# Attention, routed experts and a feed-forward block on one core: a threshold summed over all partitions, a new order in the last two batches, two id tiles and four result buffers

## The chip, the cores and the metric

The kernel runs on 1 core of one Trainium2 chip. The metric is the device time of one execution in microseconds (us); the median of the runs counts. The engines are named as in the profile: PE (TensorE, matmuls), DVE (VectorE), ACT (ScalarE), POOL (GpSimd) and SP (the queue that issues most DMAs); ACT and POOL issue DMAs too.

## The reference, cut to what matters

```python
def _attn_ref(q, k, v):                 # (8 batches, 8 heads, 576 tokens, 64)
    q_s = exp(q - max over d) / sum     # softmax over the head dimension
    k_s = exp(k - max over s) / sum     # softmax over the tokens
    kv = einsum('bhsd,bhse->bhde', k_s, v)
    return einsum('bhsd,bhde->bhse', q_s, kv)

def _moe_ref(x, w_gate, w_output_gate, w1, w2):   # x: 4608 tokens x 512, 8 experts
    logits = x @ w_gate
    e_idx = np.argmax(logits, axis=1)             # one expert for a token
    ...
    for e in range(E):
        mask = e_idx == e
        h = np.maximum(x[mask] @ w1[e], 0.0)      # 512 -> 1024
        ye = h @ w2[e]                            # 1024 -> 512
        out[mask] = gate_w[mask, None] * eom[mask, e, None] * ye

def _moe2_ref(x, w_in, w_out):                    # 512 -> 2048 -> 512
    r = np.maximum(x @ w_in, 0.0)
    return (r * r) @ w_out
```

The inputs are drawn from a seed. Drawn with the reference's own default seed, the experts get 1151, 0, 551, 25, 588, 577, 0 and 1716 tokens, and all 1151 of expert 0 are among the first 2304 tokens (batches 0 to 3).

## The kernel before, in words

**Front.** Eight batches of linear attention, two by two (a pair has 9 groups of 128 tokens). For batch n, `x_t` transposes and exponentiates q (PE, then ACT), `x_mm` multiplies by the batch's kv and the gate weights (PE, then two ACT copies), and `kv_mm`, `kv_t`, `kv_m` prepare the next batch's kv. `route_a`, `route_a1`, `route_a2`, `route_b`, `route_b2` (mostly DVE) pick each token's expert and its place in that expert's list; `scatter` (POOL, one indirect DMA for 128 tokens) writes token ids into the DRAM table `idl`. The pair before is routed while the next one is computed; the last pair is routed in two parts, `late` (4 groups) and `last` (5 groups). `crun[p, e]` counts the tokens of expert e that partition p has seen. All instructions stand in an order written by hand; each engine works its own list in that order.

**Early tokens.** While batches 6 and 7 run, the kernel takes the first 256 tokens listed for expert 0 (`early_ids`, `early_gather`, `early_scale`, `early_prep`) and, in pieces handed out by `em(1)`, multiplies them by expert 0's weights: 8 pieces of the first matmul, 8 of the second, then a store to the result `yd` in DRAM. Weights are f32, cut into two parts (`split_w1`, `split_w2`: an ACT cast, a DVE subtraction for each of 4 chunks) and every product takes three passes. `early1` is `crun[:, 0]` after batches 0 to 3. The matmul at L528 makes `pf` of it, and L535 puts 256 into `spec` where `pf` is at least 256: then 256 tokens of expert 0 count as done.

**Windows.** `window_sums` and `window_place` turn the counts, less `spec`, into a table of windows: an expert's tokens in pieces of 256, a rest of up to 128 being added to the last, which is then 384 wide. There are 25 window places; the used ones are the last of them. Places 0 to 6 are passed over by one test, places 7 to 11 have a test each, places 12 to 24 always run. A window gathers its tokens two windows ahead (ids in the tile `wid`, POOL), makes 96 matmuls of the first product (L667), 12 transposes for the next window (L661) and 96 of the second product (L675); ACT and DVE turn each of 8 first results into `h` (L669, L670). At its end ACT copies four results (L834) into `ys` and issues a store for each (L839). An expert's first window starts the load of the next expert's weights, and POOL writes each window's ids to `idc` (L687). Windows from place 12 on also carry the jobs that convert `w_in` and `w_out` for the last block.

```python
            yb = yp.tile([P, KC * TW], F32, name="yb")
            ys = [yb[:, 384 * (c % 3):384 * (c % 3) + 384] for c in range(KC)]
```

So the fourth result lies where the first does, and its copy waits for the first one's store.

**Last block.** 12 tiles of 384 tokens: L967, then L983, and a scatter of the rows to `out` (L988).

Of the kernel before, what the change touches and what calls it, by code (L numbers as in the profile page):

```python
# [83 lines left out]
def front(tc, keep, sm, cst, chf, c32, c16, ident, q, k, v, q_half, v_half, wg, wo, xd, idl, idbin, tab, moe):  # L84
# [10 lines left out]
    with ExitStack() as pctx, ExitStack() as ctx:  # L95
# [270 lines left out]
        early1 = keep.tile([P, 1], F32, name="early1")  # L366
# [102 lines left out]
        moe.split_w1([0, 1], V)  # L469
# [3 lines left out]
        route_a2(full)  # L473
        x_mm(n, 2)
# [13 lines left out]
        x_t(n, 1)  # L488
        route_a(late)
        x_mm(n, 0)  # L490
        x_t(n, 2)
        route_a1(late)
        x_mm(n, 1)
# [21 lines left out]
        em = moe.early_mm(pe, ps_t)  # L515
        spec = scratch([NE])
        V.memset(spec, 0.0)
        route_a(last)
        em(1)
        route_a1(last)  # L520
        em(1)
        route_a2(last)
        onb = rt[last][3]
# [10 lines left out]
        em(1)  # L534
        V.tensor_scalar(out=spec[:, 0:1], in0=pf, scalar1=256.0, scalar2=256.0, op0=ALU.is_ge, op1=ALU.mult)  # L535
# [40 lines left out]
def window_place(tc, t, cst, Q, tab):  # L576
# [13 lines left out]
    G.tensor_scalar(out=kk, in0=iw, scalar1=R[:, 2:3], scalar2=0.0, op0=ALU.subtract, op1=ALU.max)  # L590
    f = t([7])
# [16 lines left out]
def moe_ffn(tc, octx, ident, idbin, tab, xd, yd, idc, wid_d, w1, w2, w_in, w_out, out):  # L608
# [15 lines left out]
    def open_up():  # L624
# [5 lines left out]
        wid.append(wp.tile([P, 4], I32, name="wid"))  # L630
# [33 lines left out]
    def mm1_f(f, n, pm, h):  # L664
        for c in range(KC):
            for a, b in PASSES:
                nc.tensor.matmul(out=pm, lhsT=wA[a][:, c, f * P:(f + 1) * P], rhs=xT[b][:, c, 0:n],  # L667
                                 start=c == 0 and (a, b) == (0, 0), stop=c == KC - 1 and a == 1)
        nc.scalar.activation(out=h[0], in_=pm, func=AF.Relu)  # L669
        V.scalar_tensor_tensor(out=h[1], in0=pm, scalar=0.0, in1=h[0].bitcast(F32), op0=ALU.max, op1=ALU.subtract)  # L670
# [11 lines left out]
    def gather_tile(j, n=NT):  # L682
        nc.gpsimd.indirect_dma_start(out=xr[j], out_offset=None, in_=xd[0:n], in_offset=bass.IndirectOffsetOnAxis(ap=wid[0][:, j:j + 1], axis=0))  # L683

    def store_ids(st, n):
        with nc.allow_non_contiguous_dma(reason="token ids"):
            nc.gpsimd.dma_start(out=idc[ds(st, n * P) if n == 3 else slice(st, st + n * P), :].rearrange("(j p) o -> p (j o)", p=P), in_=wid[0][:, 0:n])  # L687

    def early_ids():
        return wid[0][:, 0:2]  # L690

    def early_gather():
        for j in range(2):
            gather_tile(j, 2 * S * EARLY)

    def early_scale():
        for j in range(2):
            scale_tile(j)
        store_ids(0, 2)
# [10 lines left out]
    def early_mm(pe, pp):  # L710
        def steps():
            for f in range(8):
                mm1_f(f, 256, pe[(f + 2) % 4][:, 0:256], [h[f] for h in hE])
# [18 lines left out]
        return go  # L732

    def gather(i):
        col = reg(i, 2, [ENG.Pool], NBIN - 1)
        nc.gpsimd.tensor_copy(out=wid[0][:, 0:3], in_=idbin[:, ds(col, 3)])
        for j in range(3):
            gather_tile(j)

    def scale(i):  # L740
# [3 lines left out]
        store_ids(st, 3)  # L744
# [8 lines left out]
    def run(regs):  # L753
# [7 lines left out]
        with ExitStack() as ctx:  # L761
# [66 lines left out]
            def mm2(i, n, st, yt, hook):  # L828
# [4 lines left out]
                for c in range(KC):  # L833
                    nc.scalar.copy(out=yt[c][:, 0:n], in_=pm[c][:, 0:n])  # L834
# [206 lines left out]
```

## Time and profile before

| | |
|---|---|
| median of 3 runs | 1571.34 us (1568.48 to 1573.19) |
| the profiled execution's own time | 1573.49 us |
| its span, first to last instruction | 1571.4 us |
| PE busy in the span | 1477.4 us (94%) |
| front, to the first window's matmul | 0 to 229.3 us |
| windows | 229.3 to 755.9 us |
| last block | from 755.9 us |

PE is busy nearly throughout, and matmuls are pipelined, so its share alone says little; what tells more is where PE starts late and what it waited for. In the rows below, a bracket at the end of a row is the idle time of that engine just before and what ended it.

### The profile page before, as it was taken

To read this page: it belongs to the slowest core of one execution; us is meant where nothing else is said; L and a number is where in the kernel's file an instruction comes from. 1 tells how busy PE (TensorE), PEld (TensorE's weight loads), DVE (VectorE), ACT (ScalarE), POOL (GpSimd) and SP (SyncE) were. 2 spreads that over 40 slices of the span, in tenths; PEclk is the share of its full clock that TensorE was granted. 3 is DMA by queue.
4 is the path that set the end of the run, shared out by engine and by line. 5 is a ranking of instruction groups with operands and counts; after the bars stand their busy time and mean duration, and the time that the engine had idled before them with its cause. 6 is when DMAs were issued, how large, how long until landed. Compare 5 with 4: busy or idle time off the path is not lost.

```text
span 1571.4 us, 24123 instructions
## 1 busy us (share of the span) xinstructions
PE 1477.4 (94%) x8993; PEld 1389.5 (88%) x8993; DVE 657.0 (42%) x1330; ACT 504.2 (32%) x1061; POOL 331.5 (21%) x350
## 2 busy tenths in 40 slices
PE   6998768999979999999799999999999999999997
PEld 6888768999979999998799999999999999999997
DVE  4466631132775566655532334323243332433322
ACT  4565511123433343433422223222232222322222
POOL 1245441322443435552100000000000000000000
PEclk9999889999989999999899999999999999999999
DMA  8574433133576756443500101010010100100000
GB/s 307 191 259 153 156 113 92 57 94 105 164 210 186 210 151 166 101 133 80 152 6 36 38 3 41 0 41 34 8 41 0 41 34 8 40 1 21 7 14 20
DMA packets 65562, 138.08 MB, mean 88 GB/s; under 512 B 13921, under 2 KB 34529, under 8 KB 61409
## 3 DMA queue, kind: packets, MB, share of 16 engines
q1 hardware_dynamic: 45456, 100.63, 21.1%
q0 software_dynamic: 9120, 24.40, 4.6%
q10 hardware_dynamic: 10800, 10.70, 2.1%
q8 instruction: 101, 1.65, 0.5%
q14 instruction: 85, 0.69, 0.2%
HBM read 101.29 MB, written 34.42 MB: 86 GB/s over the span
## 4 chain that ended last, share of the span: by engine, by line
PE 62%; DMA 4%; issue 1%; DVE 1%; ACT 1%; ACTq 0%; SPq 0%; POOLq 0%; DVEq 0%; POOL 0%
PE bank L967 25%; PE bank L983 25%; PE bank L667 7%; PE bank L675 4%; DMA raw<-moe_w 1%; DMA yb<-yd 1%; DMA cv_s<-moe_w_in 1%; PE bank L661 1%; DMA wid_d<-cv_a 0%; DMA cv_s<-moe_w_out 0%; ACTq L839 0%; DMA raw<-yd 0%; ACT yb L834 0%; DVE wA L615 0%; DMA out<-xr,idt 0%
## 5 line engine op out<-in xcount | busy, mean ns | idle before, releaser
L983 PE MATMUL bank<-wO,g 128*128 128x512 f32 x1728 | 395.8, 389 | 0.0
L983 PEld LDWEIGHTS bank<-wO,g 128*128 128x128 f32 x1728 | 324.0, 188 | 65.5
L667 PE MATMUL bank<-xT,wA 128*128 128x256 f32 (+1 forms) x1728 | 243.4, 302 | 27.1 <-ACT yb L834 16.7
L667 PEld LDWEIGHTS bank<-xT,wA 128*128 128x128 f32 x1728 | 237.7, 195 | 31.3 <-ACT yb L834 19.3
L675 PE MATMUL bank<-h,wB 128*128 128x256 f32 (+1 forms) x1728 | 235.2, 297 | 12.2 <-DVE h L670 6.6
L675 PEld LDWEIGHTS bank<-h,wB 128*128 128x128 f32 x1728 | 230.8, 192 | 13.1 <-DVE h L670 7.2
L970 ACT ACTIVATE r<-bank 128x384 f32<-128x384 f32 x192 | 94.4, 491 | 452.7 <-PE bank L967 444.5
L972 DVE TENSOR_TENSOR gg<-r 128x384 f32<-128x384 f32 x192 | 107.0, 557 | 292.2 <-ACT r L970 292.2
L967 PE MATMUL bank<-xT,wA 128*128 128x384 f32 x1152 | 209.9, 343 | 8.5 <-ACT r L970 4.6
L967 PEld LDWEIGHTS bank<-xT,wA 128*128 128x128 f32 x1152 | 207.1, 191 | 10.5 <-ACT r L970 4.9
L967 PE MATMUL bank<-xT,wB 128*128 128x384 f32 x1152 | 201.7, 334 | 0.0
L967 PEld LDWEIGHTS bank<-xT,wB 128*128 128x128 f32 x1152 | 200.1, 188 | 1.0
L988 POOL DMA_INDIRECT out<-xr,idt x36 | 35.0, 971 | 766.9 <-DVE xr L987 766.9
L615 DVE TENSOR_TENSOR g<-gg,g 128x384 fp32r<-128x384 f32 x192 | 107.1, 558 | 112.0 <-ACT g L614 112.0
L670 DVE SCALAR_TENSOR_TENSOR h<-bank,h 128x256 fp32r<-128x256 f32 (+1 forms) x144 | 59.7, 448 | 199.4 <-ACT h L669 196.6
L614 ACT CAST g<-gg 128x384 fp32r<-128x384 f32 x192 | 98.5, 513 | 121.0 <-DVE gg L972 119.8
L809 POOL TENSOR_TENSOR cv_b<-cv_b,cv_e 128x256 f32<-128x256 f32 x64 | 48.0, 751 | 199.6 <-DVE cv_b L808 199.5
L669 ACT ACTIVATE h<-bank 128x256 fp32r<-128x256 f32 (+1 forms) x144 | 53.9, 411 | 111.4 <-PE bank L667 81.8
L987 DVE COPY xr<-bank 128x512 f32<-128x512 f32 x36 | 24.9, 691 | 123.6 <-PE bank L983 123.6
L683 POOL DMA_INDIRECT xr<-xd,wid x56 | 61.7, 1102 | 55.8 <-PE bank L661 36.9
L834 ACT COPY yb<-bank 128x256 f32<-128x256 f32 (+1 forms) x68 | 27.0, 397 | 134.0 <-PE bank L675 62.7
L245 PE MATMUL px<-rx,qT 128*128 128x162 f32 x320 | 56.0, 324 | 5.8 <-ACT qT L234 5.8
(175 smaller groups left out, 1217.8 us busy)
## 6 DMA issues: line engine op xcount, KB each, us to landing
raw<-moe_w SPq DMA_DIRECT2D x52, 512.0 KB, 6.9
raw<-yd SPq DMA_DIRECT2D x11, 768.0 KB, 4.3
v<-v SPq DMA_DIRECT2D x8, 1024.0 KB, 7.5
q<-q SPq DMA_DIRECT2D x8, 1024.0 KB, 4.9
cv_s<-moe_w_in SPq DMA_DIRECT2D x32, 256.0 KB, 3.4
cv_s<-moe_w_out SPq DMA_DIRECT2D x32, 256.0 KB, 3.8
kt<-k SPq DMA_DIRECT2D x7, 1152.0 KB, 8.8
yd<-yb ACTq DMA_DIRECT2D x52, 128.0 KB, 3.1
```

The lines of the kernel that those rows point to most:

```text
L245: nc.tensor.matmul(out=px[:, c // 2, (c % 2) * 162:(c % 2) * 162 + 162], lhsT=qT[b, t][:, c, :], rhs=rx[bb % 4][:, c, :], start=True, stop ...
L614: nc.scalar.copy(out=hi, in_=src)
L615: (eng or V).tensor_tensor(out=lo, in0=src, in1=hi.bitcast(F32), op=ALU.subtract)
L667: nc.tensor.matmul(out=pm, lhsT=wA[a][:, c, f * P:(f + 1) * P], rhs=xT[b][:, c, 0:n], start=c == 0 and (a, b) == (0, 0), stop=c == KC - 1 ...
L669: nc.scalar.activation(out=h[0], in_=pm, func=AF.Relu)
L670: V.scalar_tensor_tensor(out=h[1], in0=pm, scalar=0.0, in1=h[0].bitcast(F32), op0=ALU.max, op1=ALU.subtract)
L675: nc.tensor.matmul(out=pm[c], lhsT=wB[a][:, f, c * P:(c + 1) * P], rhs=h[b], start=f == 0 and (a, b) == (0, 0), stop=f == 7 and a == 1)
L683: nc.gpsimd.indirect_dma_start(out=xr[j], out_offset=None, in_=xd[0:n], in_offset=bass.IndirectOffsetOnAxis(ap=wid[0][:, j:j + 1], axis=0))
L967: nc.tensor.matmul(out=pm, lhsT=wi(a, 8 * hf + f)[:, c], rhs=yhl[b][:, c], start=c == 0 and (a, b) == (0, 0), stop=c == KC - 1 and a == 1)
L970: nc.scalar.activation(out=r, in_=pm, func=AF.Relu)
L972: V.tensor_tensor(out=gg, in0=r, in1=r, op=ALU.mult)
L983: nc.tensor.matmul(out=pm, lhsT=g[a][:, f, u * P:(u + 1) * P], rhs=wO[b][:, 8 * hf + f, :], start=hf == 0 and f == 0 and (a, b) == (0, 0), ...
```

## The change

The threshold: `early1` becomes 16-bit, and the matmul that makes `pf` now has ones as weights, so that it sums all 128 partitions; before it took partition 0 alone, which had seen at most 18 tokens of the first 2304. The order: in batch 6 `kv_mm(7)` stands ahead of `route_a(full)`, the four chunks of `split_w1` are spread over both batches, `early_scale` stands ahead of `scatter(full)`, `load_w2` and `open_down` come later, `early_prep` comes before the last `x_mm`; the id load goes from ACT's queue to SP's; in the early product the DVE step that makes the second part of `h` is handed out apart (`st`). The tiles: two `wid` tiles in turn, four result buffers. The last window's result is stored 384 wide without a test.

```diff
-        early1 = keep.tile([P, 1], F32, name="early1")
+        early1 = keep.tile([P, 1], F16, name="early1")
...
-            nc.scalar.dma_start(out=moe.early_ids(), in_=idl[:, 0:2])
+            nc.sync.dma_start(out=moe.early_ids(), in_=idl[:, 0:2])
         x_t(n, 0)
         x_t(n, 1)
         moe.early_gather()
+        kv_mm(n + 1)
         route_a(full)
-        kv_mm(n + 1)
-        route_a1(full)
         x_mm(n, 0)
         x_t(n, 2)
         kv_t(n + 1)
-        moe.split_w1([0, 1], V)
+        route_a1(full)
         x_mm(n, 1)
         kv_m(n + 1)
         x_t(n, 3)
         route_a2(full)
+        moe.early_scale()
+        moe.split_w1([0], V)
         x_mm(n, 2)
         route_b(full)
         route_b2(full)
         scatter(full)
         x_mm(n, 3)
-        moe.split_w1([2, 3], V)
-        rctx.close()
-        moe.open_down()
-        moe.early_open()
-        moe.early_scale()
-        moe.load_w2(0)
...
         x_mm(n, 2)
         x_t(n, 4)
         route_b(late)
+        moe.split_w1([3], V)
+        rctx.close()
+        moe.open_down()
+        moe.early_open()
+        moe.load_w2(0)
         x_mm(n, 3)
         route_b2(late)
         scatter(late)
-        moe.split_w2([0, 1], V)
+        moe.early_prep(ps_t)
         x_mm(n, 4)
-        moe.early_prep(ps_t)
...
-        em = moe.early_mm(pe, ps_t)
+        em, st = moe.early_mm(pe, ps_t)
...
-        nc.tensor.matmul(out=pf, lhsT=ident[:, 0:1].to_broadcast([P, P]), rhs=early1, start=True, stop=True)
+        nc.tensor.matmul(out=pf, lhsT=chf[:, H_1:H_1 + P], rhs=early1, start=True, stop=True)
+        st(1)
+        route_b(last)
         em(1)
-        route_b(last)
+        st(1)
+        moe.split_w2([0], V)
         route_b2(last)
         scatter(last)
...
-        window_place(tc, scratch, cst, wq, tab)
         em(1)
-        moe.split_w2([2], V)
-        em(1)
-        moe.split_w2([3], V)
+        st(1)
...
+        window_place(tc, scratch, cst, wq, tab, mid)
+        st(1)
+        moe.split_w2([1, 2, 3], V)
         moe.gather(MAXW)
-        em(2)
+        em(4)
         moe.scale(MAXW)
-        em(4)
         regs = moe.regs()
         em(2)
...
-        wid.append(wp.tile([P, 4], I32, name="wid"))
+        wid.extend(wp.tile([P, 3], I32, name=f"wid{i}") for i in range(2))
...
-                    nc.scalar.copy(out=yt[c][:, 0:n], in_=pm[c][:, 0:n])
+                    w = n if i < MAXW - 1 else TW
+                    nc.scalar.copy(out=yt[c][:, 0:w], in_=pm[c][:, 0:w])
...
-            ys = [yb[:, 384 * (c % 3):384 * (c % 3) + 384] for c in range(KC)]
+            ys = [yb[:, TW * c:TW * (c + 1)] for c in range(KC)]
...
-            with tc.If(v_ == 3) as br:
-                for c in range(KC):
-                    store(384, st, c, yt[c])
-            with br.Else():
-                for c in range(KC):
-                    store(256, st, c, yt[c])
+            st, yt = late[0]
+            for c in range(KC):
+                store(384, st, c, yt[c])
```

On ACT, where batch 5's last copies (L248, L249) end and batch 6's first exponentials (L234) begin, one piece of the difference:

```order
 L248 COPY xt_even<-px 64x512
 L249 COPY lp_even<-px 64x136
-L459 DMA wid<-idl 128x2
 L234 ACTIVATE qT<-pt 128x512 x2
 L248 COPY xt_odd<-px 128x512
```

The id load is gone from ACT; it now stands on SP behind the four loads of `raw`.

On DVE in batch 6, the routing of `full` (L258 to L273) and the kv of batch 7 (L170 to L180). Before:

```order
L258 TENSOR_SCALAR rc<-lp_even 128x72
L259 RECIPROCAL rc<-rc 128x72
L261 TENSOR_TENSOR lp<-lp_even,rc 128x1152
L170 TENSOR_SCALAR ks<-ks 128x4
L171 RECIPROCAL ks<-ks 128x4
L180 TENSOR_TENSOR rx_108<-px,ks 64x4x64 x2
L269 TENSOR_REDUCE lg<-lp 128x144
```

And now:

```order
L170 TENSOR_SCALAR ks<-ks 128x4
L171 RECIPROCAL ks<-ks 128x4
L180 TENSOR_TENSOR rx_108<-px,ks 64x4x64 x2
L258 TENSOR_SCALAR rc<-lp_even 128x72
L259 RECIPROCAL rc<-rc 128x72
L261 TENSOR_TENSOR lp<-lp_even,rc 128x1152
L269 TENSOR_REDUCE lg<-lp 128x144
```

The multiply L261 moved behind L180, which needs the matmuls of `kv_mm`.

On DVE in the routing of `last`, from its weight (L307 to L311) to its place numbers (L333 to L343), with the early product's second parts `he`. Before:

```order
L311 TENSOR_TENSOR xt_odd<-rc,eo 128x5x8
L333 TENSOR_SCALAR ea<-m_1812 128x5
L335 TENSOR_TENSOR ro<-pt,onb 128x40
L337 TENSOR_REDUCE rs<-ro 128x5
L339 CAST ri<-rs 128x5
```

And now:

```order
L311 TENSOR_TENSOR xt_odd<-rc,eo 128x5x8
L685 SCALAR_TENSOR_TENSOR he_3_1686<-pe_1761,he_3_1678 128x256
L629 TENSOR_TENSOR wB_1668<-raw,wB_1667 128x1024
L333 TENSOR_SCALAR ea<-m_1822 128x5
L335 TENSOR_TENSOR ro<-pt,onb 128x40
L337 TENSOR_REDUCE rs<-ro 128x5
```

A residual of the early product and a chunk of `w2` (L629, `split_w2([0])`) moved ahead of the place numbers, on which `scatter(last)` waits.

## Rows read from the trace of the kernel before

**Rows 1.** Last block: length; busy PE, PEld, DVE, ACT, POOL; granted clock; DMA share

```profile
785.00:1564.00 779.00, 778.21 (x3937) 710.35 (x3935) 252.53 (x421) 202.42 (x384) 34.00 (x35) 1.00 0.06 22
```

**Rows 2.** Groups by line and shape: first product, both widths

```profile
L667 PE MATMUL bank<-xT,wA 128*128 128x256 f32 x1344 | 173.7, 291 | 24.5 <-ACT yb L834 15.5 <-issue 7.9 <-DVE h L670 1.0
...
L667 PE MATMUL bank<-xT,wA 128*128 128x384 f32 x384 | 69.7, 340 | 2.6 <-DVE h L670 1.5 <-ACT yb L834 1.1
```

**Rows 3.** Timeline of PE in the windows: start, us, instruction, idle before

```profile
229.29 14.25 PE L667 MATMUL bank<-xT,wA 128*128 128x256 f32 x96 [7.92 <-issue]
...
255.90 5.92 PE L667 MATMUL bank<-xT,wA 128*128 128x256 f32 x48
266.40 8.84 PE L667 MATMUL bank<-xT,wA 128*128 128x256 f32 x48 [4.58 <-ACT yb L834]
...
287.59 5.91 PE L667 MATMUL bank<-xT,wA 128*128 128x256 f32 x48
296.38 7.65 PE L667 MATMUL bank<-xT,wA 128*128 128x256 f32 x48 [2.88 <-ACT yb L834]
...
316.39 10.94 PE L667 MATMUL bank<-xT,wA 128*128 128x384 f32 x60
...
354.74 11.75 PE L667 MATMUL bank<-xT,wA 128*128 128x256 f32 x96 [1.99 <-ACT yb L834]
...
628.43 11.68 PE L667 MATMUL bank<-xT,wA 128*128 128x256 f32 x96
...
652.47 11.68 PE L667 MATMUL bank<-xT,wA 128*128 128x256 f32 x96
```

**Rows 4.** Timeline of ACT at the end of the first window

```profile
257.58 2.60 ACTq L839 DMA_DIRECT2D yd<-yb  x1
265.97 0.37 ACT L834 COPY yb<-bank 128x256 f32<-128x256 f32 x1 [8.43 <-DMA yd<-yb]
```

**Rows 5.** Waits between 416 and 756 us: total, times, longest

```profile
PE bank L675 <- DVE h L670: 6.6, 3, 4.0
PE bank L667 <- ACT yb L834: 6.6, 5, 2.9
```

**Rows 6.** Timelines of ACT (first row) and PE in batches 6 and 7

```profile
154.26 1.08 ACT L234 ACTIVATE qT<-pt 128x512 f32<-128x512 f32 x2 [9.13 <-DMA idl<-cst,ri]
...
154.91 2.53 PE L245 MATMUL px<-rx,qT 128*128 128x162 f32 x8 [3.44 <-ACT qT L234]
...
164.48 0.21 PE L326 MATMUL pt<-onb,chf 128*128 128x72 f16 x1 [1.42 <-DVE onb L289]
...
169.35 1.81 PE L245 MATMUL px<-rx,qT 128*128 128x162 f32 x8 [2.36 <-ACT qT L234]
...
182.10 0.65 PE L661 MATMUL pt<-ident,xr 128*128 128x128 f32 x4 [2.67 <-POOL xr L680]
```

**Rows 7.** Timeline of POOL: batch 7's subtraction, and the last scatter

```profile
152.58 3.63 POOL L220 TENSOR_TENSOR qe<-q,qm 128x2048 f32<-128x2048 f32 x1
...
197.56 0.96 POOL L349 DMA_INDIRECT idl<-cst,ri  x1 [8.69 <-DVE ri L343]
```

**Rows 8.** Timeline of DVE: a subtraction of `route_a1(full)`, and the routing of `last`

```profile
154.78 2.52 DVE L273 TENSOR_TENSOR dl<-lg,mx 128x72 f32<-128x72 f32 x1
...
185.03 0.17 DVE L258 TENSOR_SCALAR rc<-lp_odd 128x40 f32<-128x40 f32 x1
...
188.32 0.42 DVE L670 SCALAR_TENSOR_TENSOR he<-pe,he 128x256 fp32r<-128x256 f32 x1 [1.82 <-ACT he L669]
...
194.44 0.42 DVE L670 SCALAR_TENSOR_TENSOR he<-pe,he 128x256 fp32r<-128x256 f32 x1 [2.10 <-ACT he L669]
```

**Rows 9.** Groups by line and shape on DVE

```profile
L615 DVE TENSOR_TENSOR wB<-raw,wB 128x1024 fp32r<-128x1024 f32 x23 | 35.2, 1577 | 3.2 <-ACT wB L614 3.2
...
L273 DVE TENSOR_TENSOR dl<-lg,mx 128x72 f32<-128x72 f32 x3 | 3.0, 995 | 0.1
...
L261 DVE TENSOR_TENSOR lp<-lp_even,rc 128x1152 f32<-128x1152 f32 x2 | 2.7, 1358 | 0.1
```

More of the change, by code (lines that the diff above doesn't have):

```diff
@@ L488, in front @@
         x_t(n, 1)
+        moe.split_w1([1], V)
         route_a(late)
@@ L492, in front @@
         route_a1(late)
+        moe.split_w1([2], V)
         x_mm(n, 1)
@@ L534, in front, with mid @@
         em(1)
+        st(1)
         V.tensor_scalar(out=spec[:, 0:1], in0=pf, scalar1=256.0, scalar2=256.0, op0=ALU.is_ge, op1=ALU.mult)
         window_sums(tc, scratch, cst, pc, spec, wq)
-        window_place(tc, scratch, cst, wq, tab)
         em(1)
-        moe.split_w2([2], V)
-        em(1)
-        moe.split_w2([3], V)
+        st(1)
+        def mid():
+            em(1)
+            st(1)
+        window_place(tc, scratch, cst, wq, tab, mid)
+        st(1)
+        moe.split_w2([1, 2, 3], V)
         moe.gather(MAXW)
-        em(2)
+        em(4)
         moe.scale(MAXW)
-        em(4)
         regs = moe.regs()
@@ L573, in window_sums, with window_place @@
     V.tensor_copy(out=Q[:, 1, 0:1], in_=full[:, 0:1])
-def window_place(tc, t, cst, Q, tab):
+def window_place(tc, t, cst, Q, tab, mid):
     G = tc.nc.vector
@@ L590, in window_place @@
     G.tensor_scalar(out=kk, in0=iw, scalar1=R[:, 2:3], scalar2=0.0, op0=ALU.subtract, op1=ALU.max)
+    mid()
     f = t([7])
@@ L668, in mm1_f, with residual @@
                                  start=c == 0 and (a, b) == (0, 0), stop=c == KC - 1 and a == 1)
+    def residual(pm, h):
+        V.scalar_tensor_tensor(out=h[1], in0=pm, scalar=0.0, in1=h[0].bitcast(F32), op0=ALU.max, op1=ALU.subtract)
+    def mm1_f(f, n, pm, h):
+        mm1_pe(f, n, pm)
         nc.scalar.activation(out=h[0], in_=pm, func=AF.Relu)
-        V.scalar_tensor_tensor(out=h[1], in0=pm, scalar=0.0, in1=h[0].bitcast(F32), op0=ALU.max, op1=ALU.subtract)
+        residual(pm, h)
     def mm2_f(f, pm, h):
@@ L698, in early_scale @@
             scale_tile(j)
-        store_ids(0, 2)
+        store_ids(1, 0, 2)
     def early_open():
@@ L710, in early_mm @@
     def early_mm(pe, pp):
+        left = []
         def steps():
             for f in range(8):
-                mm1_f(f, 256, pe[(f + 2) % 4][:, 0:256], [h[f] for h in hE])
+                h = [x[f] for x in hE]
+                pm = pe[(f + 2) % 4][:, 0:256]
+                mm1_pe(f, 256, pm)
+                nc.scalar.activation(out=h[0], in_=pm, func=AF.Relu)
+                left.append((pm, h))
                 yield
@@ L731, in go, with st @@
                 next(it)
-        return go
+        def st(n):
+            for _ in range(n):
+                residual(*left.pop(0))
+        return go, st
     def gather(i):
         col = reg(i, 2, [ENG.Pool], NBIN - 1)
-        nc.gpsimd.tensor_copy(out=wid[0][:, 0:3], in_=idbin[:, ds(col, 3)])
+        nc.gpsimd.tensor_copy(out=wid[i % 2][:, 0:3], in_=idbin[:, ds(col, 3)])
         for j in range(3):
-            gather_tile(j)
+            gather_tile(i, j)
     def scale(i):
@@ L743, in scale @@
             scale_tile(j)
-        store_ids(st, 3)
+        store_ids(i, st, 3)
     engs = [ENG.PE, ENG.Activation, ENG.DVE, ENG.SP, ENG.Pool]
@@ L923, in slot @@
                 if last:
-                    late.append((v_, st, yt))
+                    late.append((st, yt))
             def guarded(lo, hi, vs=None):
@@ L940, in run @@
             load_y(1, yr[1])
-            v_, st, yt = late[0]
-            with tc.If(v_ == 3) as br:
-                for c in range(KC):
-                    store(384, st, c, yt[c])
-            with br.Else():
-                for c in range(KC):
-                    store(256, st, c, yt[c])
+            st, yt = late[0]
+            for c in range(KC):
+                store(384, st, c, yt[c])
         with ExitStack() as ctx:
```

16 lines of the change are left out of this document (9 added, 7 removed).

## The prediction

> **What bounds the kernel now.** I read the busy time by stretch first. [...]
>
> The groups by line come next. The first product has 1344 matmuls of 256 columns and 384 of 384 in the windows [rows 2], and a window has 96: 14 narrow and 4 wide windows, 18 in all. The counts of the reference's own seed give the same 18: expert 0 with 1151 tokens takes (1151 + 127) / 256 = 4 (the last one wide), the others 2, 1, 2, 2 and 7. They would be 17 if 256 tokens of expert 0 counted as done. So the early product, made in full on PE, is thrown away and its tokens are multiplied again.
>
> Then PE's timeline [rows 3]. A late, undisturbed narrow window lasts 652.47 - 628.43 = 24.0 us. The first four, all expert 0's, start at 229.29, 255.90, 287.59 and 316.39, the fifth at 354.74: 26.6, 31.7, 28.8 and (wide) 38.4 us. In the second and third PE stands still halfway, for 4.58 and 2.88 us, on a result copy, and the 48 matmuls behind the stop take 8.84 and 7.65 us where 48 take 5.92 ahead of it. ACT's timeline says why: its fourth copy waited 8.43 us for a store from the same buffer, and the next window's `h` stand behind it in ACT's queue [rows 4].
>
> Last the front, where PE, DVE, ACT and POOL wait for each other in turn [rows 6, 7, 8].
>
> **The sum, part by part.** It is made against the profiled execution's own 1573.49 us, which lies 2.15 us above the median of the runs.
>
> *The window that goes.* With `pf` summed over all partitions it is 1151, at least 256, so `spec` becomes 256 and expert 0 has 895 tokens: (895 + 127) / 256 = 3 windows, the last still wide. The places used are then 8 to 24, and all windows after expert 0 keep their kind and their work. What stays is a first window (26.6), a second and the wide one, so a 28.8 us window goes; if the disturbance moved over to the one that stays, only 24.0. I take **-28.8**. The two 16-bit operands of `pf` cost nothing: one tiny matmul in place of another.
>
> *Four result buffers.* The fourth copy no longer waits for a store of its own window, but for one of the window before, made some 24 us earlier. In the window that stays the excess goes: 31.69 - 24.04 = **-7.65**. Lower bound nothing: one of ACT's own store issues stood 2.60 us [rows 4], so the queue can hold ACT up as well; I take the whole, because 257.58 + 2.60 and a copy's length end near 261 us, and PE needs that bank at 255.90 + 5.92 = 261.8 [rows 3]. From 416 us on, PE waited 6.6 us for such copies and 6.6 us for `h`, which stand behind them [rows 5]. Some of that is due to weights that arrive late, not to the buffer, so of 13.2 I take **-5** (0 to 13.2). Two id tiles: POOL's wait for an id store ended ahead of its wait for PE in every window of expert 0, so they are worth nothing there; if they delayed a gather, 12 us of second product would cover it.
>
> *The front.* ACT stood 9.13 us in front of batch 6's exponentials, since the id load in its queue waited for scatters; PE lost 3.44 us by it [rows 6]. On SP only stores stand behind that load, and their data come later. But `route_a(full)` now stands behind `kv_mm(7)`, so its own multiply of 1.36 us [rows 9] starts only when that is through on PE, which puts it inside POOL's subtraction from 152.58 to 156.21 and a shorter one behind it [rows 7]. In this trace one such DVE operation, with two tensors read from SBUF, fell into that stretch: 2.52 us, to 157.30, where the other two of its group share 0.5 [rows 8, 9]. So I let the multiply wait to the same end: 157.3 + 1.36, then an estimated 4 us of the steps behind it, and PE has its operand near 162.7; before, it had it at 164.48 after waiting [rows 6]. The 2.36 us wait at 169.35 goes with the casts that stood ahead of it, which makes PE some 1.8 + 1.7 = 3.5 us early (part of the 2.36 remains, since the exponential itself has to be waited for). Three `w1` casts and two `xT` casts then stand between batch 7's copies on ACT, which gives about 2 back. `route_a(last)` started at 185.03 [rows 8], held up by the early tokens' scaling behind `scatter(full)` (PE's 2.67 us wait at 182.10 [rows 6]); with the scaling moved ahead it starts near 180.6, that is 4.4 earlier. From there to `scatter(last)` at 197.56 [rows 7], DVE stood idle 1.82 and 2.10 us for first halves of `h` [rows 8] that now are a piece ahead; against that it does one chunk of `w2`, 1.58 [rows 9]. So the last scatter comes some 7 us earlier, and after it the same things follow: table, gather, scaling, and 8 pieces of the second product on PE. **-7**, between 0 (all taken back by the new order) and -11 (without the wait of the multiply, which costs 4).
>
> [...]
>
> *The seventh place.* PE idled 7.92 us before the first window [rows 3] with its data there: the program passes over places 0 to 6, and then inside place 7 over the wide form. Now place 7 is empty, and its test is one more pass over some 400 rows. Two passes in 7.92 us make 3.96 each, so **+4**; at least nothing, since inside the windows passes over 96 matmuls leave no gap (652.47 starts without one), at most 7.92.
>
> [...]
>
> *At no cost.* The 384-wide store of the last window adds 128 columns to four ACT copies and takes a test away. `load_w2`, later by some 5 us on SP, is covered by the routing of `last`; uncovered it is the second rival.
>
> Sum: -28.8 - 7.65 - 5 - 7 + 4 = -44.5; 1573.49 - 44.5 = 1529.0, and against the median **1527 us**.
>
> **The rivals.**
>
> *The copies still wait.* The stores drain slowly whatever the buffer, and ACT is held up at its issues, as once for 2.60 us. Against it: 8.43 us of the stop are put down to the buffer's own store. Terms -7.65 and -5 fall away: 1527 + 12.6 = 1540.
>
> *The front comes no earlier.* The first chunk of `w2` now stands on DVE ahead of the place numbers of `last`. `load_w2` is issued behind the store of `late` and the last `w1` chunk; if it lands later than some 187 us, the delay goes through scatter and gather to the first window. Against it: some 10 us lie between issue and need. The 7 us are gone: 1534.
>
> *The threshold does nothing.* If the chip's inputs are others, with fewer than 256 early tokens for expert 0, 18 windows stay. For the seed speaks that the widths in the trace are those it gives. Left are -7 - 7.65 - 4.76 (the third window's excess) - 5: 1547.
>
> *Slower.* The last block runs at a lower granted clock. The block's 779 us at 1.00 would have to be granted 779 / (779 + 44.5) = 0.946 on the mean; below that the kernel is slower than before, at 0.94 by some 5 us (1577). Against it: nothing in its rows changes, and it runs with no gap.
>
> **How the numbers follow.** Forecast 0.60 (its own range 1515 to 1537), copies still wait 0.14, front no earlier 0.19, threshold does nothing 0.05, slower 0.02. Range: the unknown prices (-24.0 to -28.8, 0 to -7.65, 0 to -13.2, 0 to -11, 0 to +7.9) seldom fall on one side together; down, a larger share of the 13.2 and of the front give 1513; up, the first two rivals, with part of the place's upper price, 1543. Outside lie the last two rivals and what the tails hold, 0.2. Under 0.3%, 4.7 us, a measurement of this kernel can't tell from no change. All cases but the last end far below: faster 0.97, same 0.01, slower 0.02.
>
> **What would show it.** First product 1248 matmuls of 256 columns instead of 1344; no 4 us stop of PE on a result copy in expert 0's windows; no ACT copy waiting for a store; the first window's matmul near 226 us (229.29 - 7 + 4) behind a pause of some 12 us; the early tokens' transposes without a wait for POOL; the last block as before. It would be wrong if 1344 stood there, if the stop moved to `h`, or if the pause ahead of the first window grew past 16 us.

## The result, and the profile after

The changed kernel takes 1526.94 us (median of 4 runs, 1523.15 to 1536.90) where the kernel before, on the same chip, takes 1571.31 (4 runs): a ratio of 0.9729, 95% interval 0.9681 to 0.9777 (this ratio and all below are of the means of the runs). The forecast was 1527. The profiled execution took 1523.15 us (span 1521.5, before 1571.4), the fastest of the four, and that of the kernel before 1573.49, so differences of the two profiles add up to 49.9 us where the medians differ by 44.4.

The groups by line and shape, the answer to [rows 2] (the line number has moved from 667 to 681):

```profile
L681 PE MATMUL bank<-xT,wA 128*128 128x256 f32 x1248 | 156.7, 288 | 21.9 <-ACTq L960 13.4 <-ACT yb L865 8.2 <-ACT wA L628 0.3
L681 PE MATMUL bank<-xT,wA 128*128 128x384 f32 x384 | 68.2, 338 | 0.0
```

96 narrow matmuls are gone, one narrow window. The waits on copies (`ACT yb`) have fallen from 15.5 to 8.2 us, but the idle time in front of the first window has grown: 13.4 us.

PE's timeline in the windows, the answer to [rows 3]:

```profile
228.68 12.89 PE L681 MATMUL bank<-xT,wA 128*128 128x256 f32 x96 [13.44 <-ACTq L960]
...
254.03 11.56 PE L681 MATMUL bank<-xT,wA 128*128 128x256 f32 x96
...
277.94 17.05 PE L681 MATMUL bank<-xT,wA 128*128 128x384 f32 x96
...
313.11 11.55 PE L681 MATMUL bank<-xT,wA 128*128 128x256 f32 x96
...
337.02 17.05 PE L681 MATMUL bank<-xT,wA 128*128 128x384 f32 x96
...
372.19 0.52 PE L681 MATMUL bank<-xT,wA 128*128 128x256 f32 x3
```

Expert 0 has three windows of 25.4, 23.9 and (wide) 35.2 us, none with a stop in its middle, and the third window of all starts at 313.11 with no wait, where [rows 3] has 1.99 us on a copy. Why the stops are gone is in ACT's waits (total, times, longest): in the kernel before its copies stood 47.9 us for a store from their own buffer, and the changed kernel's list has no such wait at all. Before:

```profile
ACT yb L834 <- DMA yd<-yb: 47.9, 17, 8.4
```

The run cut into stretches, with the columns of [rows 1] and GB/s at the end. First the changed kernel: the pause ahead of the first window, the windows up to the 13th place, the other windows, a stretch of the last block. Then the first three of the kernel before:

```profile
215.23:228.68 13.45, 0.01 (x2) 0.03 (x1) 0.61 (x2) 0.37 (x1) 6.53 (x8) 0.60 0.71 122
228.68:372.19 143.51, 143.51 (x1021) 143.44 (x1021) 50.92 (x97) 44.30 (x91) 41.04 (x43) 0.99 0.45 121
372.19:707.78 335.59, 316.90 (x2437) 313.86 (x2437) 216.94 (x505) 132.64 (x297) 156.07 (x175) 0.98 0.60 160
735.00:1514.00 779.00, 778.15 (x3935) 709.35 (x3934) 253.00 (x422) 203.05 (x386) 33.99 (x35) 1.00 0.06 22
```

```profile
221.37:229.29 7.92, 0.00 (x1) 0.03 (x1) 0.60 (x2) 0.37 (x1) 3.20 (x5) 0.71 0.45 106
229.29:416.17 186.88, 175.33 (x1225) 173.05 (x1226) 55.66 (x108) 49.92 (x106) 51.30 (x54) 0.96 0.33 104
416.17:755.88 339.71, 319.00 (x2438) 316.05 (x2437) 210.49 (x505) 130.60 (x296) 153.67 (x175) 0.97 0.58 158
```

So the front gave 0.6 us (229.29 to 228.68, where the prediction had 226), the windows up to the 13th place 43.4, the others 4.1 and the last block 1.8, which makes 49.9. Within the front two things nearly cancel: the early product ends 6.1 us earlier (221.37 to 215.23), and the pause behind it is 5.5 us longer. It is the only stretch that got worse, with DMA engines 0.71 busy for only 122 GB/s.

### The profile page after: what moved, and what is told of

It is laid out like the page before. It is cut to its first block, busy times and chain, and to the rows that moved or that the text cites. A ratio compares the mean times of both kernels' runs of the same rounds, so it can differ in the third digit from the quotient of the medians.

```text
span 1521.5 us, 23570 instructions
## 1 busy us (share of the span) xinstructions
PE 1438.1 (95%) x8788; PEld 1351.0 (89%) x8788; DVE 659.5 (43%) x1319; ACT 500.2 (33%) x1046; POOL 328.0 (22%) x342
## 4 chain that ended last, share of the span: by engine, by line
PE 73%; DMA 5%; DVE 3%; issue 2%; ACT 1%; SPq 0%; ACTq 0%; POOLq 0%; DVEq 0%; POOL 0%
PE bank L994 25%; PE bank L1010 25%; PE bank L681 12%; PE bank L695 10%; DMA raw<-moe_w 2%; DMA wid_d<-cv_a 2%; PE bank L675 1%; DMA yb<-yd 1%; ACT wB L628 1%; DVE wB L629 0%; DVE wA L629 0%; SPq L657 0%; DVE cv_a L829 0%; DMA raw<-yd 0%; ACT g L628 0%
## 5 line engine op out<-in xcount | busy, mean ns | idle before, releaser
L681 PE MATMUL bank<-xT,wA 128*128 128x256 f32 (+1 forms) x1632 | 224.9, 300 | 21.9 <-ACTq L960 13.4
L681 PEld LDWEIGHTS bank<-xT,wA 128*128 128x128 f32 x1632 | 221.9, 193 | 23.4 <-ACTq L960 13.6
L695 PE MATMUL bank<-h,wB 128*128 128x256 f32 (+1 forms) x1632 | 220.9, 296 | 10.2 <-issue 5.5
L695 PEld LDWEIGHTS bank<-h,wB 128*128 128x128 f32 x1632 | 215.9, 190 | 11.9 <-issue 6.7
L994 PEld LDWEIGHTS bank<-xT,wA 128*128 128x128 f32 x1152 | 205.5, 190 | 8.2 <-ACT r L997 3.9
L629 DVE TENSOR_TENSOR g<-gg,g 128x384 fp32r<-128x384 f32 x192 | 107.2, 558 | 112.2 <-ACT g L628 112.2
L825 ACT ACTIVATE cv_m<-cv_s 128x256 f32<-128x256 f32 x64 | 28.1, 439 | 96.3 <-DVE cv_a L833 55.6
L700 POOL TENSOR_TENSOR xr<-xr 128x512 f32<-128x512 f32 x53 | 55.5, 1069 | 15.0 <-DMA xr<-xd,wid 14.5
```

What stands on the lines that cost most here:

```text
L629: (eng or V).tensor_tensor(out=lo, in0=src, in1=hi.bitcast(F32), op=ALU.subtract)
L695: nc.tensor.matmul(out=pm[c], lhsT=wB[a][:, f, c * P:(c + 1) * P], rhs=h[b], start=f == 0 and (a, b) == (0, 0), stop=f == 7 and a == 1)
L700: nc.gpsimd.tensor_tensor(out=xv, in0=xv, in1=xr[j][:, DM:XW].unsqueeze(2).to_broadcast([P, H, D]), op=ALU.mult)
L994: nc.tensor.matmul(out=pm, lhsT=wi(a, 8 * hf + f)[:, c], rhs=yhl[b][:, c], start=c == 0 and (a, b) == (0, 0), stop=c == KC - 1 and a == 1)
```

## The experiments

Each kernel ran in turn with the kernel before on one chip; the sets ran on different chips, where that takes 1578.5 us (the first four below), 1587.6 (old order, first quarter, one id tile, the changed kernel again), 1573.8 (projection behind the routing, first id store behind, the same with the seventh place) and 1580.3 (first id store ahead), so ratios are compared. A difference of 0.001 is 1.6 us; most intervals are plus or minus 0.003.

### The threshold alone

In the kernel before:

```diff
-early1 = keep.tile([P, 1], F32, name="early1")
+early1 = keep.tile([P, 1], F16, name="early1")
-nc.tensor.matmul(out=pf, lhsT=ident[:, 0:1].to_broadcast([P, P]), rhs=early1, ...)
+nc.tensor.matmul(out=pf, lhsT=chf[:, H_1:H_1 + P], rhs=early1, ...)
```

> The kernel before with the summed threshold alone (16-bit early1, ones as weights of pf); all else as before. Theory A (the sum's own terms): one narrow window goes, 24.0 to 28.8 us, with 1248 matmuls of 256 columns left in the first product, and the pause ahead of the first window grows by 4 to 5.5 us for the empty seventh place; in total 19 to 25 us less than before, some 1549. The stops of PE on a result copy stay in the second window. Theory B (most of the gain is the order and the buffers): 10 us less or fewer.

Ratio 0.9833 (0.9807 to 0.9858): 26.4 us less, with 1248 narrow matmuls. That is the window that goes less what the empty place costs. With the front and the tiles as before, the pause ahead of the first window grew from 7.92 to 11.02 us, 3.1 us and not 4 to 5.5:

```profile
235.87 14.63 PE L667 MATMUL bank<-xT,wA 128*128 128x256 f32 x96 [11.02 <-ACTq L929]
```

### All but the threshold

The same lines the other way round, in the changed kernel.

> The changed kernel with the old threshold (partition 0 alone). Theory A: 18 windows again, the added one undisturbed since four buffers stay, +23.9, and the pause ahead of the first window back to some 8 us, -5.5: some 18 us above the changed kernel, 1545. Theory B: 10 us or less above it. If the pause stays at 13 us in spite of a full seventh place, the empty place is not its cause, and something else that the change brought is (the earlier gather of the second window, whose transfers lie in the pause).

Ratio 0.9860 (0.9825 to 0.9895), 1344 narrow matmuls. Against the changed kernel (0.9729, and 0.9716 in a later set) the threshold is worth 21 to 23 us here. That is less than the 26.4 alone, but within the intervals; a smaller worth would fit, since a window without stops is shorter (23.9 us against 28.8). The pause is 9.52 us: with the seventh place in use it is 4 to 5 us shorter than the changed kernel's.

```profile
233.41 12.95 PE L681 MATMUL bank<-xT,wA 128*128 128x256 f32 x96 [9.52 <-DVEq L963]
```

### Three result buffers

```diff
-ys = [yb[:, TW * c:TW * (c + 1)] for c in range(KC)]
+ys = [yb[:, 384 * (c % 3):384 * (c % 3) + 384] for c in range(KC)]
```

> The changed kernel with three result buffers (the fourth copy again shares the first one's). Theory A: PE stops again halfway in the windows behind the first: places 8 to 12 take 152 to 156 us in place of 143.5, and some 4 us come on top behind them: 1527 + 12 to 17 = 1541. Rival (the stop came from slow stores, not from the shared buffer): within 3 us of the changed kernel.

Ratio 0.9804 (0.9775 to 0.9834): the fourth buffer is worth 12 to 14 us, with some 8 us of noise either way. Places 8 to 12 take 154.5 us (238.42 to 392.94) in place of 143.5, as theory A has it, and ACT's copies stand 43.9 us for stores again (47.9 in the kernel before). PE's timeline in expert 0's second window has the old stop, as [rows 3] at 266.40:

```profile
264.18 5.86 PE L681 MATMUL bank<-xT,wA 128*128 128x256 f32 x48
273.43 8.83 PE L681 MATMUL bank<-xT,wA 128*128 128x256 f32 x48 [3.38 <-ACT yb L865]
```

### The seventh place in the common test

Places 0 to 7 are passed over in one jump, not 0 to 6 in one and 7 in another (the register of the common test moves by one place with it, not shown):

```diff
-guarded(0, SKIP // 2 + 1)
+guarded(0, SKIP // 2 + 2)
-guarded(SKIP // 2 + 1, SKIP, vs)
+guarded(SKIP // 2 + 2, SKIP, vs)
```

> The changed kernel with place 7 put under the one test that passes over places 0 to 6, so that the empty place is not passed over on its own. Theory A (the pause holds one pass over code for each test): the pause ahead of the first window falls from 13.4 us to 8 to 9.5, the kernel to 1522 or so. Rival (the pause is long because transfers of the second window's gather lie in it): the pause stays above 12 us.

Ratio 0.9706 (0.9681 to 0.9731): 1.6 to 3.6 us below the changed kernel's, inside the intervals; the pause is 9.71 us, a little above theory A's range and far from the rival's.

```profile
236.36 13.77 PE L681 MATMUL bank<-xT,wA 128*128 128x256 f32 x96 [9.71 <-DVEq L963]
```

### The old order of the front

The threshold, the id tiles, the buffers and the stores stay; the rest of the front is put back, among others

```diff
-kv_mm(n + 1)
 route_a(full)
+kv_mm(n + 1)
...
-moe.split_w2([0], V)
 route_b2(last)
```

> The changed kernel with the front in the old order (projection of pair 7 and routing steps, splits of the weights, early tokens' work and the second products where they stood before); the summed threshold, the two id tiles, the four result buffers and the empty seventh place stay. Theory A (my sum: the new order is worth 7 us at the end of the early product, and nothing else depends on it): the last scatter starts 3 to 4 us later after the last routing step, the early product ends 6 us later against its own start, and the time is 5 to 7 us above the changed kernel run beside it (ratio to the kernel before 0.976 to 0.978 if that stands at 0.973). Rival (the pause ahead of the first window is set by transfers and code that don't wait for the early product): the pause shrinks by what the product is late, and the time is within 2 us of the changed kernel's. The first window's own length and the windows behind it should not differ by either.

Ratio 0.9775 (0.9742 to 0.9807), beside 0.9716 for the changed kernel in the same set: 9.4 us more, though the two intervals overlap. The last scatter starts at 197.68 (194.96 there), the early product ends at 221.50 (216.34), and the pause does not shrink. PE's timeline:

```profile
235.99 1.41 PE L667 MATMUL bank<-xT,wA 128*128 128x256 f32 x5 [14.49 <-ACTq L930]
241.11 12.87 PE L667 MATMUL bank<-xT,wA 128*128 128x256 f32 x91 [3.71 <-issue]
```

The first window starts 5.2 us later than at 230.81. Behind its fifth matmul comes a second stop of 3.71 us, which no theory had. So by the profiles the order is worth some 5 us by itself.

### The projection behind the routing again

```diff
-kv_mm(n + 1)
 route_a(full)
+kv_mm(n + 1)
```

> The changed kernel with the first routing step of the fifth pair's full blocks ahead of the next pair's key-value projection, as before the change. Theory A (in the changed kernel VectorE's first routing operation falls under GpSimd's subtraction, 4.49 us in place of 0.2, and TensorE waits 6.2 us for the routing's one-hot): with the routing first the wait is 1 to 3 us, but the projection then comes later on TensorE; the early product ends 0 to 4 us earlier and the time is 0 to 4 us below the changed kernel's. [...]

Ratio 0.9723 (0.9696 to 0.9751), the changed kernel's. PE's wait for the one-hot fell from 6.17 to 1.42 us, the early product ended at 214.38 (215.23 and 216.34 in the two profiles of the changed kernel), and the pause is 14.20. Of the 4.75 us that this wait got shorter, 0.9 to 2.0 are left at the end of the early product and none in the time.

### The first quarter of the second weights behind the scatter

```diff
-moe.split_w2([0], V)
 route_b2(last)
...
-moe.split_w2([1, 2, 3], V)
+moe.split_w2(range(KC), V)
```

> The changed kernel with the split of the first quarter of expert 0's second weights moved from ahead of the last routing step to behind the window sums, in front of the other three quarters. Theory A (the split stands in VectorE's queue ahead of the last row indices, where it waited 1.75 us for ScalarE and took 1.2 us): the last scatter starts 2.5 to 3 us earlier (against the end of the routing's first part), the ids reach the window tiles that much earlier, the second products of the early tokens come behind the split and are no later at their end, and the first window starts up to 3 us earlier: time 0 to 3 us below. Rival (the second products want that quarter before the rest): the first piece of the second product is 5 us or more later, the early product ends later, the pause shrinks by as much or the first window comes later: time 0 to 4 us above.

Ratio 0.9711 (0.9683 to 0.9739): no difference. The last scatter does start 2.75 us earlier (192.21), and the early product ends at 215.89, 0.45 earlier; but the pause is 20.50 us, and the first window starts at 236.39, 5.6 us later than the changed kernel's 230.81; neither theory has a pause that grows.

```profile
236.39 14.34 PE L680 MATMUL bank<-xT,wA 128*128 128x256 f32 x96 [20.50 <-issue]
```

What the pause consists of was the next question.

### One id tile

```diff
-wid.extend(wp.tile([P, 3], I32, name=f"wid{i}") for i in range(2))
+wid.append(wp.tile([P, 4], I32, name="wid"))
...
```

(`wid[0]` stands wherever the changed kernel has `wid[i % 2]`.)

> The changed kernel with one id tile as before, so that the second window's gather can't start until the first window's ids are stored. Theory A (the gather that two tiles let into the pause ahead of the first window holds up the loads of code there): the pause shrinks from 13.4 us by 1.5 to 2 us, the first window starts that much earlier, and the second window's transposes wait or don't; the time is 1 to 2 us below the changed kernel's, or the same where the second window waits. Rival (the transfers are hidden in the pause, its length is the branch alone): the pause stays 13 to 14 us, the gather ends 8 us later, the second window waits for it or not at all, and the time is the same or up to 5 us above.

Ratio 0.9738 (0.9708 to 0.9768), the same. The second gather is issued at 224.50 (217.68 with two tiles), and a third of its bytes move behind the pause, yet the pause is 15.63 us. So theory A, by which it shrinks, fell; two thirds of the gather still lie in this pause, so that what a gather in it costs is not measured here.

### The changed kernel again

> The changed kernel itself, without any edit, for a direct comparison on the chip of the other three. Ratio to the kernel before 0.973 again (0.970 to 0.976). If the hole of 5 to 7 us ahead of the early product that the first four variants showed belongs to their edits, it is not here; if it belongs to the chip, it is here too and in the kernel before as well.

Ratio 0.9716 (0.9675 to 0.9757), pause 14.47 us (230.81), and no hole ahead of the early product; the hole is taken up at the end.

```profile
230.81 14.13 PE L681 MATMUL bank<-xT,wA 128*128 128x256 f32 x96 [14.47 <-ACTq L960]
```

### The first id store behind the second window's

Two theories were left for the pause: the loads of code that the jumps bring, and the store of the first window's ids (384 elements of 4 bytes), which starts 2.8 us ahead of it and takes 8 to 11. In the store's line, `held` keeps the first window's and issues it with the second's:

```diff
 def scale(i):
-    st = reg(i, 1, [ENG.Pool], NT - 1)
+    held.append((i, reg(i, 1, [ENG.Pool], NT - 1)))
     for j in range(3):
         scale_tile(j)
-    store_ids(i, st, 3)
+    if i == MAXW:
+        return
+    for k, st in held:
+        store_ids(k, st, 3)
+    held.clear()
```

> The changed kernel with the store of the first window's ids (384 elements of 4 bytes) issued right ahead of the second window's, behind the second window's scaling, that is some 15 us later and no longer in the pause ahead of the first window. Theory A (in the pause the loads of code and the second gather queue behind these small elements: 13.4 us with a DMA share of 0.71 at only 122 GB/s): the second gather lands in 4 to 6 us instead of 8 to 9, the pause falls from 13.4 to 14.5 us to 9 to 11, the first window starts 3 to 5 us earlier against the early product's end, and the time is 3 to 5 us below the changed kernel's (ratio about 0.969 if that stands at 0.972). Rival 1 (the pause is the number of code loads that the jump over the empty place brings, whatever else moves): the pause stays at 13 to 15 us and the time is the same. Rival 2 (the stores then fall into the first window and hold up its code): the pause shrinks and the first window shows stops of as much, time the same.

Ratio 0.9708 (0.9690 to 0.9725): the same within the intervals. The pause falls to 10.07 us, 4.4 less than in the changed kernel's second profile, and the first window, 26.5 us there, now takes 31.2, with a stop in its second product:

```profile
230.02 14.16 PE L681 MATMUL bank<-xT,wA 128*128 128x256 f32 x96 [10.07 <-issue]
...
253.17 8.17 PE L695 MATMUL bank<-h,wB 128*128 128x256 f32 x56 [2.82 <-issue]
```

Rival 2 holds: what the pause gains, the window loses.

### The same, with the seventh place in the common test

> Both edits together: the first window's id store behind the second window's scaling, and the empty seventh place back in the common test of the empty places. Theory A (small elements and code loads each lengthen the pause): the pause falls to 6 to 8 us (9.7 us with the place in the common test alone), and the time is 5 to 8 us below the changed kernel's. If only the jump counts: 9 to 10 us and 4 us below. If only the small elements count, it is no better than the edit of the store alone. It would be faster than both kernels.

Ratio 0.9701 (0.9681 to 0.9722). The two edits add up in the pause, 5.68 us, the shortest of all, and again the first window gives it back; the first product ends at 234.23, and the next row stands behind 7.71 us:

```profile
220.93 13.30 PE L681 MATMUL bank<-xT,wA 128*128 128x256 f32 x96 [5.68 <-issue]
241.94 2.79 PE L675 MATMUL bank<-ident,xr 128*128 128x128 f32 x12 [7.71 <-DMA xr<-xd,wid]
```

The releaser named can't be right, since POOL had scaled those rows by 224.3; what PE waited for there stays open.

### The first id store ahead of the scaling

The seventh place in the common test, and

```diff
+if i == MAXW:
+    store_ids(i, st, 3)
 for j in range(3):
     scale_tile(j)
-store_ids(i, st, 3)
+if i != MAXW:
+    store_ids(i, st, 3)
```

> The changed kernel with the empty seventh place in the common test of the empty places, and with the first window's ids stored ahead of its three scalings in GpSimd's order, some 4 us earlier, so that its small elements are through before the pause has to load code. Theory A (small elements hold up whatever queues behind them, code above all): the store lands 4 us earlier, the pause is 6 to 8 us (9.7 us with the place alone, 5.7 us with the store moved behind), the first window shows no stop as the later store gave it (25 to 26.5 us), and the time is 3 to 6 us below the changed kernel's: ratio 0.967 to 0.969. Rival (the elements only change places: now they hold up the first window's scalings or the gather's last rows): the transposes ahead of the pause wait 3 us or more, the early product's end moves by as much, and the ratio stays at 0.970.

Ratio 0.9704 (0.9681 to 0.9728). The pause is 8.31 us and the first window 26.7, but the transposes ahead of the pause now wait for the scaling:

```profile
223.83 0.66 PE L675 MATMUL pe<-ident,xr 128*128 128x128 f32 x4 [2.19 <-POOL xr L700]
```

The rival holds: the 2.2 us move to the other side of the pause. No version is clearly faster than the changed kernel; the four that shorten the pause stand at 0.970 to 0.971 against its 0.972 to 0.973, but so does the one with the longest pause (0.971), so that the ratios don't settle it.

## What the pause is made of

Early product's end, pause and first window (stops in it included) are from PE's timelines; the code loads are the packets of the two instruction queues in the pause (16 KB ones + 8 KB ones; with the old order to the end of its second stop).

| kernel | early product ends | pause | code loads | first window |
|---|---|---|---|---|
| before (place 7 in use) | 221.37 | 7.92 | 1 + 4 | 26.6 |
| all but the threshold (in use) | 223.89 | 9.52 | 1 + 2 | 25.3 |
| place 7 in the common test | 226.65 | 9.71 | 1 + 2 | 26.1 |
| the same, store behind | 215.25 | 5.68 | 1 + 3 | 35.2 |
| the same, store ahead | 228.73 | 8.31 | 1 + 4 | 26.7 |
| changed | 215.23 | 13.44 | 3 + 5 | 25.4 |
| changed, again | 216.34 | 14.47 | 3 + 7 | 26.5 |
| threshold alone | 224.85 | 11.02 | 3 + 6 | 27.0 |
| three buffers | 224.38 | 14.04 | 3 + 5 | 25.8 |
| projection behind routing | 214.38 | 14.20 | 3 + 7 | 26.1 |
| one id tile | 214.97 | 15.63 | 3 + 6 | 27.9 |
| store behind | 219.95 | 10.07 | 3 + 7 | 31.2 |
| old order | 221.50 | 14.49 + 3.71 | 3 + 9 | 30.4 |
| first quarter behind scatter | 215.89 | 20.50 | 3 + 9 | 27.4 |

The place that is empty and tested by itself brings two more loads of 16 KB in every kernel that has it, and in none that hasn't. Between kernels otherwise alike that is 9.7 us against 13.4 and 14.5 with the store in the pause, and 5.7 against 10.1 with the store behind it. The DMA queues of the changed kernel's second profile in its pause (packets, MB, share of 16 engines; the store line's last number is us to landing), then of the kernel with the store behind and place 7 in the common test:

```profile
q8 instruction: 3, 0.05, 5.1%
q14 instruction: 7, 0.06, 3.8%
yd<-ye SPq DMA_DIRECT2D x4, 128.0 KB, 9.9
```

```profile
q14 instruction: 3, 0.02, 1.5%
q8 instruction: 1, 0.02, 1.5%
yd<-ye SPq DMA_DIRECT2D x4, 128.0 KB, 4.5
```

A 128 KB store on another queue lands in 9.9 us beside the small elements and in 4.5 without them; the test of the seventh place differs too between these two kernels. The second gather shows the same in the profiles of all fourteen kernels of the table. From its first issue to POOL's first scaling of it pass 8.4 to 10.0 us in the eight kernels that issue it some 4 us behind the start of the id store, and 4.1 to 6.0 in the six where that store has landed, was issued earlier or comes later. POOL in the changed kernel's second profile, then in the kernel with the store behind and place 7 in the common test:

```profile
217.68 0.98 POOL L703 DMA_INDIRECT xr<-xd,wid  x1 [0.61 <-PEq L963]
...
227.55 3.04 POOL L700 TENSOR_TENSOR xr<-xr 128x512 f32<-128x512 f32 x3 [6.37 <-DMA xr<-xd,wid]
```

```profile
215.57 1.00 POOL L703 DMA_INDIRECT xr<-xd,wid  x1 [0.60 <-PE pe L695]
...
220.98 1.04 POOL L700 TENSOR_TENSOR xr<-xr 128x512 f32<-128x512 f32 x1 [1.88 <-DMA xr<-xd,wid]
```

That the loads of code are held up in the same way fits the pause's fall of 4.0 and 4.4 us, but no view shows a load's own wait.

Pause and first window together show what remains: 34.5 to 35.8 us in four of the five kernels that don't test an empty place by itself, 38.0 to 47.9 in the nine that do. With the store behind they are 40.9 (place in the common test) and 41.2, no less than the changed kernel's 38.8 and 41.0.

## Why the prediction was right, and where it was off

*The window that goes, -28.8, and the seventh place, +4: right.* The threshold alone gave 26.4 us where the two make 24.8. The place's 4 us is the 3.7 to 4.8 between a pause with and without it (9.71 against 13.44 and 14.47), and 3.1 where the threshold alone empties it. The working, 7.92 us as two passes of 3.96 each, is not borne out: with the store out of the way two passes stand in 5.68 us and a third makes that 10.07, so that the two parts of 7.92 were not passes alone, and that 3.96 came near is in part luck. What goes with the place in the table is two more loads of 16 KB of code in the pause, 3 against 1.

*Four result buffers, -7.65 and -5: right in sum, 12 to 14 us measured (12.65 expected).* In the profile the gain lies otherwise. The second window and the one that goes took 36.6 us less (36.45 expected). From 416 us on it was 4.1 (5 expected), since ACT still copies late: the waits of PE from 372 to 708 us have 8.2 and 2.6 us for the 6.6 and 6.6 of [rows 5]:

```profile
PE bank L681 <- ACT yb L865: 8.2, 5, 3.8
PE bank L695 <- issue: 5.5, 6, 2.4
PE bank L695 <- DVE h L685: 2.6, 1, 2.6
```

Left out were the windows in between: expert 0's last and the two behind it took 5.5 us less (3.2 and 2.35), by the 1.99 us wait of [rows 3] and smaller ones. With 1.3 us in the first window that makes the 43.4; this last 1.3 is not the change's, since the second profile of the changed kernel has 26.5 us there for the 26.6 before.

*The front, -7: 5 to 6, for partly other reasons.* The early product ends 6.1 us earlier, and with the old order the first window starts 5.2 later. Of the 6.1 us only 0.6 reached the first window; the longer pause took the rest, some 4 of it for the seventh place. The steps on the way, in the timelines of PE (first row), DVE (two rows) and POOL (three):

```profile
163.77 0.24 PE L326 MATMUL pt<-onb,chf 128*128 128x72 f16 x1 [6.17 <-DVE onb L289]
```

```profile
152.73 4.49 DVE L258 TENSOR_SCALAR rc<-lp_even 128x72 f32<-128x72 f32 x1
...
182.08 0.17 DVE L258 TENSOR_SCALAR rc<-lp_odd 128x40 f32<-128x40 f32 x1
```

```profile
152.53 3.63 POOL L220 TENSOR_TENSOR qe<-q,qm 128x2048 f32<-128x2048 f32 x1
156.11 1.05 POOL L224 TENSOR_TENSOR qh<-qh,qm 128x512 f32<-128x512 f32 x1
...
194.09 0.96 POOL L349 DMA_INDIRECT idl<-cst,ri  x1 [5.92 <-DVE ri L343]
```

The operation that meets POOL's subtraction [rows 7] is not the multiply, as forecast, but the one ahead of it, which adds a constant: 4.49 us, to 157.22, where it took 0.18 with the routing first. It stood through both of POOL's subtractions, the second of which follows the first at once and ends at 157.16. The time came out as forecast, 157.3, and PE had its operand at 163.8 (162.7): there PE is only 0.7 us ahead of the kernel before, since this wait took back most of what the moved id load had given. The forecast went by an operation that reads two tensors ([rows 8], 2.52 us); the one that stood here reads one, `lp_even`. Why it took 4.49 us, no run shows. `route_a(last)` started at 182.08 (180.6 expected), and the last scatter came 3.5 us earlier, not 7: the first quarter of the second weights waited 1.75 us for ACT and took 1.23 on DVE right ahead of the row numbers. Before, the early product's end didn't hang on that scatter, as the prediction had it, but on PE's own order: PE made its late transposes at 217.08 with no wait for POOL. Its second half now starts 7.2 us earlier. PE before, then now:

```profile
201.26 1.23 PE L675 MATMUL pt<-he,wB 128*128 128x256 f32 x9
...
217.08 1.04 PE L661 MATMUL pe<-ident,xr 128*128 128x128 f32 x8
```

```profile
194.10 1.21 PE L695 MATMUL pt<-he,wB 128*128 128x256 f32 x9
...
209.87 0.66 PE L675 MATMUL pe<-ident,xr 128*128 128x128 f32 x4 [0.47 <-POOL xr L700]
211.32 0.66 PE L675 MATMUL pe<-ident,xr 128*128 128x128 f32 x4 [0.80 <-POOL xr L700]
```

3.2 us of that come ahead of the first half, where the transposes no longer wait for the early scaling ([rows 6], 2.67 us); 4.0 come within it (12.9 us, before 16.8). By the late transposes PE is 7.8 us ahead. There it meets POOL's scaling, which came 3 us earlier only, and loses 1.7 us again around the two waits: now the scatter counts too.

*The pause, "some 12 us": 13.4 and 14.5.* This is the term that was undersized. The 4 us of the place are as forecast; the 1.5 to 2.5 above them are the step "after it the same things follow". They did not keep their distance: the early product ended 6.1 us earlier, the store of the first window's ids only 2.9 (215.29 to 212.43), so more of it lay in the pause. That the store costs some 4 us there is shown by the runs with it moved (4.0 and 4.4); that its shift makes up these 1.5 to 2.5 us is only argued.

*The rivals.* "The copies still wait" is out (three buffers bring the stop back, four don't have it, nor any copy that waits for a store); "the front comes no earlier" is out by the run with the old order; "the threshold does nothing" by the count of 1248 and the three windows of expert 0; and the last block ran at a granted clock of 1.00, 778.15 of 779.00 us busy, as [rows 1].

*The sum.* That 1527 was met to 0.1 us is luck: the four runs spread over 13.8 us. In the profiles the windows gave 6.8 us more than their terms (5.5 in windows that were left out, 1.3 in the first) and 0.9 less from 416 us on, the front and the pause together 2.4 less, and the last block 1.8 that no term had. The two large terms, the window and the buffers, are each shown by a run of their own.

## What to carry to other kernels

Where two chains meet at one point (here a product and the transfers that prepare what follows), pulling one forward can slide it into the other's tail (the product ended 6.1 us earlier here, and 0.6 of it reached the first window): ask what else ends near the new time, not only what the step itself saves. The store of 384 small elements took 8 to 11 us here, and the pause was 4.0 and 4.4 us shorter without it; two other places were tried, and each gave back what it gained: behind the pause the first window took 31.2 and 35.2 us for 26.5 and 26.1, ahead of the scaling the transposes waited 2.19 us. When a table empties a slot, look at how the empty slot is passed over: here that took 3.7 to 4.8 us.

## What the runs showed that was not expected

- 384 elements of 4 bytes (1.5 KB) take 8 to 11 us to land, and a 128 KB store on another queue then lands in 9.9 instead of 4.5 us.
- The pause costs again afterwards: its granted clock is 0.60 on the mean, the first product behind it ran at 0.89 (0.50 up to 231.5 us, 1.00 from there on) and took 12.7 us, that of the second window ran at 1.00 and took 11.4. The cost does not follow the pause's length: before, behind 7.92 us, the first product took 14.1 at 0.80. Both stretches of the changed kernel, in the columns of the table by stretch:

```profile
228.68:241.41 12.73, 12.73 (x97) 12.73 (x98) 2.97 (x7) 2.69 (x7) 0.55 (x2) 0.89 0.28 79
254.03:265.42 11.39, 11.39 (x99) 11.39 (x97) 2.69 (x7) 3.48 (x10) 0.00 (x0) 1.00 0.37 46
```

- With the old order or the first quarter moved, the 8 KB code loads rise to 9 and the waits to 18 and 20 us, though no more branches are taken. The threshold alone has the old order too, with 6 such loads and 11.0 us. What makes the difference, no run shows.
- In all profiles of the first and the last set PE stood 5.5 to 7.2 us just ahead of the early product (with the threshold alone, ahead of batch 7's last two `x_mm`), for something the profile doesn't name; in the nine other profiles it did not. The kernel with three buffers has the changed kernel's front instruction for instruction and has it, the changed kernel hasn't, twice; so it goes with the chip or the hour, not with an edit. Its cause stays open.
